# Element-wise work on either of two engines, one weight ring for all chunks, and a rearranged start, in a fused attention and MLP kernel

## The chip, the cores and the metric

The kernel runs on one core of a Trainium2 chip. The metric is the device time of one launch in microseconds. Five engines work side by side, each through its own list of instructions in order: PE (TensorE, matmuls; PEld is its weight load), DVE (VectorE), ACT (ScalarE), POOL (GpSimd) and SP (SyncE, which here only issues DMAs). An instruction that waits for a semaphore holds back everything behind it on its engine.

## The reference

One transformer block on a sequence of 2048 rows and 512 columns, 32 heads of 16, in float32:

```python
mod = (_silu(c) @ w_mod).reshape(c.shape[0], 6, 1, -1)
sa, ca, ga, sb, cb, gb = (mod[:, 0], mod[:, 1], mod[:, 2], mod[:, 3], mod[:, 4], mod[:, 5])
h = _layernorm(x, axis=-1) * (1 + ca) + sa
x = x + ga * _A_ref(h, A_wqkv, A_wo)             # softmax attention, 32 heads, then @ wo
h = _layernorm(x, axis=-1) * (1 + cb) + sb
x = x + gb * _B_ref(h, B_w1, B_w2, B_w3, B_w4)
```

`_B_ref` is two parts with residuals: `gelu(layernorm(x) @ w1)`, whose four column quarters are shifted by 1, -1, 2 and -2 rows and multiplied by `w2`; then `gelu(layernorm(x1) @ w3) @ w4` with 1792 hidden columns. The matrices are scaled up by 8 or 64, so plain bfloat16 products are not accurate enough.

## The kernel before

**Numbers in two parts.** Each matmul operand is kept as a high part and a low part (`hi = Copy(x)` on ACT, `lo = x - hi` by a subtraction), and a product is three matmuls: hi·hi, hi·lo, lo·hi (`mm3`, L322, L324 and L326 of the helper).

**Prologue (about the first 107 us).** The first layer norm, its transposes `hT`, the modulation columns, and the first group of K and Q columns. Q, K and V go to DRAM (`Qs`, `Ks`, `Vs`) and come back per head pair.

**Attention.** The sequence is cut into four chunks of 512 query rows; a chunk has 16 head pairs; a head pair in a chunk is a *unit* (64 units, the `units` list) of 16 key tiles, so there are 1024 steps `s`. A step has for each of two heads:

- `mb` (L939, PE) and `mx` (L935, DVE, `reduce_max` of a 128x512 bank): the row maxima, taken 24 steps ahead (`LEAD`),
- `sc` (L955, PE) and `pt` (L951, ACT, `Exp` into int32): the scores. The maximum is part of the matmul, through rows of `qtl` written by the DMAs `qtl<-nm`,
- the low half of P (`p_low`, L1003): one POOL instruction of 128x1024 for both heads, or two of 128x512 on ACT (`L120` in the profile) when the planner sees POOL more than `LACT` = 800 ns behind ACT,
- `pv` (L1028 high part, L1025 low part, PE).

**Fillers.** Everything else is written as Python generators that yield PE time, and as chains of element-wise steps `("A" | "D" | "G", cost, function)`, with A for ACT, D for DVE and G for POOL. They are: Q, K and V of the later heads; the weights of the MLP and of `wo`, split once into two parts and stored to DRAM as 20 pieces of 1 MB (`pieces_load`, `pieces_gen`; buffers `wst` and `wq`); the modulation rows `garow`, `sbrow`, `cbrow` and `gbrow` (`mod_gen`); and per chunk a `tail`: `wo`, two layer norms, `w1` with gelu, `w2`, `w3` with gelu, `w4`. The tail of the last chunk runs after attention.

**What sets the order.** `Sched` writes the program in the order of a planned time. It has a time for each engine (`T`), a cost for each step (`cA`, `cD`, `cG`: for DVE `n/0.96 + 69` ns, for POOL `2.2 n + 40` ns), and places the fillers between blocks of attention by a budget per step. `misc(e, until)` puts the ready steps of chains into the plan of engine `e`; `crit` places the steps of attention. The order that comes out is fixed in the program; on the chip each engine follows its list and waits on semaphores. The planner's costs are constants: a DVE step has the same cost whatever POOL is doing at that moment. Seven PSUM banks (`NSM`) are shared by scores, maxima and fillers, so a bank that DVE or ACT has not read yet holds up the next matmul.

**Gelu in the attention stage.** Its chain is: ACT square and copy (L1311, L1312), DVE cube (L1316, with one operand in PSUM), ACT tanh and scale (L1320, L1321), POOL product `xs<-xs,sq` (L1322), ACT high part (L1306), POOL low part `g<-xs,g` (L1307). After attention the product is on DVE (L1328) and only the low part on POOL.

**The tail's weights** come through a `Ring` of three 1 MB buffers `wr`, made anew in each `tail`; `get` takes loaded pieces and `more` asks for the next when the matmuls on them are planned.

Of the kernel before, what the change touches and what calls it, by code (L numbers as in the profile page):

```python
# [21 lines left out]
P = 128  # L22
KT = D // P
NKT = S // P
CH = 512
# [33 lines left out]
LACT = 800.0  # L59
WX = 2  # L60
# [4 lines left out]
PLOAD = 3500.0  # L65
WSR = 1
# [10 lines left out]
class Sched:  # L77
# [57 lines left out]
    def misc(self, e, until):  # L135

        while True:
            best = None
            for ch in self.chains:
                if ch[1] and ch[1][0][0] == e:  # L140
                    start = max(self.T[e], ch[0])
                    if ch[3] in self.owner and ch[0] <= max(until, self.T[e]):
                        best = start, ch
                        break
                    if start + ch[1][0][1] <= until + AGE * max(0.0, self.T[e] - ch[0]) and (not best or start < best[0]):
                        best = start, ch
            if not best:
                break
            self.emit(best[1])

    def emit(self, ch):

        e, cost, fn = ch[1].pop(0)
# [140 lines left out]
def kernel(ctx, tc, A_x, A_wqkv, A_wo, B_w1, B_w2, B_w3, B_w4, c, w_mod, out):  # L294
# [7 lines left out]


# [496 lines left out]

    def pieces_load():
        yield lambda: ("v", 0, 2) in done
        for i, (nm, src, nk, n) in enumerate(pieces):
            if i == order["wo"][0]:
                yield lambda: ("vcol", 0) in done and ("vcol", 1) in done
                yield from mod_gen((2, garow, 0.0))
            if i == order["w4"][0]:
                yield lambda: len(wqs) == NWQ and not loaded
                yield from mod_gen((3, sbrow, 0.0), (4, cbrow, 1.0), (5, gbrow, 0.0))
            src3 = kpn(src)  # L810
            for c in range(2):
# [3 lines left out]
                loaded.append((i, nm, c, t, e))  # L815
        loaded.append(None)

    def pieces_gen():
        while True:
# [11 lines left out]
            if nm in rows:  # L831
                ops.append(("G", cG(), lambda f=f, r=rows[nm]: pool.tensor_tensor(f, f, r, op=OP.mult)))
# [5 lines left out]
            def store(i=i, c=c, w=w, f=f, gone=gone):  # L838
                for h, t in enumerate((w.bitcast(F32), f)):
                    e = sch.dma(dma.dma_start, Ws[i][:, h, 512 * c:512 * c + 512], t)  # L840
                sch.after(e, gone)
            sch.chain(*ops, ("A", cA(), lambda f=f, w=w: act.activation(w, f, AF.Copy)),
                      ("G", cG(), lambda f=f, t=t, w=w: pool.tensor_tensor(t, f, w, op=OP.subtract)),
                      (None, 0, store), ready=e)
        yield lambda: len(wqs) == NWQ
# [26 lines left out]
    for g in (mod_cols(), bounds(), ln1_T(), qk_first(hi, lo), weights_gen(), qkv_gen(0, 3), qkv_gen(1, 2, 4, 5, 6)):  # L872
# [118 lines left out]
    def p_low(s):  # L991
# [4 lines left out]
        g, a = [max(sch.T[e], ready) for e in "GA"]  # L996
        if g > a + LACT:
# [12 lines left out]
    def pv_part(s, lo):  # L1010
# [20 lines left out]
        if lo:  # L1031
# [3 lines left out]
            if kt % 4 == 2:  # L1035
                load_v(u + 1, kt // 4)
# [42 lines left out]
    tp = [None, None]  # L1079

    class Ring:


        def __init__(self, ids):
# [3 lines left out]
            self.add(3)  # L1088

        def add(self, n, pl=0):  # L1090

            for _ in range(n):
                if self.n < len(self.ids):
# [3 lines left out]
                    sch.dma(dma.dma_start, w.bitcast(F32), Ws[i])  # L1097
                    self.q.append((halves(w, pieces[i][2]), pl))
# [53 lines left out]
    def tail(ci):  # L1152
# [10 lines left out]
        ids = order["wo"] + order["w1"] + order["w2"]  # L1163
        for f0, nf in FG:
            ids = ids + order["w3"][f0 // 2:(f0 + nf) // 2] + order["w4"][f0 // 2:(f0 + nf) // 2]
        ring = Ring(ids)
# [17 lines left out]
        wo, more = ring.get(2)  # L1184
# [73 lines left out]
        for i, t in enumerate(new):  # L1258
# [16 lines left out]
            def center(xb=xb, x1=x1, m=m, ops=ops):  # L1275
                ops[0][2]()
                sch.late = sch.put("G", 464, sch.T["D"] - cD() + XX, ops[1][2]) + XX
# [5 lines left out]
            go = partial(sch.chain, ("D", cD(), x1_add), ("D", 2 * cD() + 150, center), ("D", cD(), scale), *ops2,  # L1283
# [9 lines left out]
        def gelu(b, n, hi, lo, key):  # L1293
# [8 lines left out]
            def end():  # L1302
# [4 lines left out]
                        ("G", cG(n), lambda: pool.tensor_tensor(lo, xs, hi, op=OP.subtract)), (None, 0, end))  # L1307
            if psd["s"]:
# [6 lines left out]
                def cube():  # L1315
# [6 lines left out]
                          ("G", cG(n), lambda: pool.tensor_tensor(xs, xs, sq, op=OP.mult)), *tail_ops, bank=b)  # L1322
# [21 lines left out]
        for gi, ts in enumerate(grp):  # L1344
# [4 lines left out]
            for half in range(2):  # L1349
                if gi == 0:  # L1350
                    w1.append(ring.get(1))
# [10 lines left out]
        w, more = ring.get(2)  # L1362
# [208 lines left out]
```

## Time and profile before

| | |
|---|---|
| median of 3 runs | 2130.53 us (2129.33 to 2140.78) |
| profiled execution | 2136.83 us, its span 2135.1 us |
| granted PE clock, mean | 0.963 |
| busy: PE, PEld | 1977.7 us (93%), 1163.4 us (54%) |
| busy: DVE, ACT, POOL | 1647.3 us (77%), 1544.9 us (72%), 1708.3 us (80%) |
| DMA | 292.68 MB in 228513 packets |

Busy PE time is a loose measure, since matmuls are pipelined and their ends are modelled. Busy shares over the whole span are means over stages with different limits: the prologue to 107 us, an early part of attention to 499 us in which Q, K, V and the weight pieces are made, the rest of attention to 1945 us, and the last tail. A time in the trace is counted from the start of the span.

### The profile page before, as it was taken

What the parts mean: (1) busy time and instruction counts of PE and PEld (TensorE: products, weight loads), DVE (VectorE), ACT (ScalarE), POOL (GpSimd) and SP (SyncE); (2) the same over time, 40 slices, a digit from 0 to 9 for tenths busy, and PEclk for the clock granted to TensorE, in tenths of its full rate; (3) what the DMA queues carried; (4) which work ended last, traced back from release to release, by engine and by line L of the source; (5) the groups of instructions that cost most, each with busy time, mean ns of one, the idle gap of its engine ahead of it and who ended that gap; (6) DMA issues with size and microseconds to landing.
All of it is one profiled execution on the core that took longest, in us unless ns stands there. A gap on an engine that the chain in (4) does not pass through costs nothing.

```text
span 2135.1 us, 41502 instructions
## 1 busy us (share of the span) xinstructions
PE 1977.7 (93%) x14464; PEld 1163.4 (54%) x14464; DVE 1647.3 (77%) x2936; ACT 1544.9 (72%) x3336; POOL 1708.3 (80%) x1649
## 2 busy tenths in 40 slices
PE   6979898999898999999989999999899999998899
PEld 4645554554343555555444555555545555555788
DVE  6758678788779888878888888788798888861654
ACT  5367777668866878877867897887678887785353
POOL 4378788679987999988968999898779998896441
PEclk9989999999887999999989999999989999999899
DMA  5787867656564344454543444445543434443332
GB/s 193 196 256 222 225 176 204 166 151 167 166 182 99 80 121 105 121 129 124 162 99 68 108 113 124 109 112 124 149 102 82 129 87 107 122 114 118 147 139 84
DMA packets 228513, 292.68 MB, mean 137 GB/s; under 512 B 121264, under 2 KB 172976, under 8 KB 212016
## 3 DMA queue, kind: packets, MB, share of 16 engines
q1 hardware_dynamic: 228304, 290.02, 49.9%
q8 instruction: 115, 1.88, 0.4%
q14 instruction: 94, 0.77, 0.1%
HBM read 226.49 MB, written 62.91 MB: 136 GB/s over the span
## 4 chain that ended last, share of the span: by engine, by line
PE 54%; DVE 14%; ACT 12%; DMA 8%; POOL 7%; issue 3%; SPq 3%; POOLq 0%; ACTq 0%; DVEq 0%
PE mb L939 11%; PE pv L1028 8%; DVE mx L935 8%; PE sc L955 8%; ACT pt L951 6%; PE w L324 5%; PE w L322 5%; PE w L326 5%; POOL pt L1003 4%; PE pv L1025 4%; SPq L99 3%; DMA qtl<-nm 2%; DMA wst<-in_w_mod_dram 1%; DMA wst<-in_B_w_dram 1%; DVE tst L333 1%
## 5 line engine op out<-in xcount | busy, mean ns | idle before, releaser
L935 DVE TENSOR_REDUCE mx<-mb 128x1 f32<-128x512 f32 x2048 | 1280.9, 683 | 208.2 <-PE mb L939 176.5
L1003 POOL TENSOR_SCALAR pt<-pt 128x1024 f16<-128x1024 uint16 x975 | 1300.2, 1367 | 148.1 <-ACT pt L951 145.0
L951 ACT ACTIVATE pt<-sc 128x512 int32<-128x512 f32 x2048 | 1081.7, 607 | 305.5 <-PE mb L939 230.6
L939 PE MATMUL mb<-kst,qtl 48*128 48x512 f32 x2048 | 779.1, 464 | 73.7 <-ACT pt L951 35.9
L955 PE MATMUL sc<-qtl,kst 64*128 64x512 f32 x2048 | 744.4, 456 | 31.7 <-DMA qtl<-nm 16.6
L939 PEld LDWEIGHTS mb<-kst,qtl 48*128 48x128 f32 x2048 | 354.8, 197 | 290.0 <-ACT pt L951 108.8
L955 PEld LDWEIGHTS sc<-qtl,kst 64*128 64x128 f32 x2048 | 344.1, 190 | 202.3 <-ACT pt L951 62.5
L1028 PE MATMUL pv<-pt,vst 128*32 128x512 f16 x4096 | 366.2, 405 | 0.0
L1025 PE MATMUL pv<-pt,vst 128*25 128x512 f16 (+1 forms) x2048 | 214.3, 403 | 0.5 <-POOL pt L1003 0.5
L1028 PEld LDWEIGHTS <-vst 128*32 128x32 bf16 x4096 | 92.1, 96 | 165.0 <-issue 109.7
L322 PE MATMUL w<-A,wr 128*128 128x256 f32 (+2 forms) x576 | 173.4, 301 | 3.2 <-ACT A L316 3.0
L1307 POOL TENSOR_TENSOR g<-xs,g 128x256 fp32r<-128x256 f32 (+2 forms) x144 | 103.8, 722 | 87.7 <-ACT g L1306 87.5
L324 PE MATMUL w<-A,wr 128*128 128x256 f32 (+2 forms) x576 | 172.3, 299 | 1.3 <-DVE A L312 1.1
L326 PE MATMUL w<-A,wr 128*128 128x256 f32 (+2 forms) x576 | 170.1, 295 | 0.0
L322 PEld LDWEIGHTS w<-A,wr 128*128 128x128 f32 x576 | 111.4, 193 | 22.3 <-issue 11.8
L324 PEld LDWEIGHTS w<-A,wr 128*128 128x128 f32 x576 | 111.3, 193 | 19.1 <-issue 16.3
L322 PE MATMUL w<-wr,g 128*128 128x512 f32 x288 | 119.4, 415 | 1.7 <-DVE x L1407 0.9
L326 PE MATMUL w<-wr,g 128*128 128x512 f32 x288 | 118.2, 411 | 0.5 <-POOL g L1307 0.3
L326 PEld LDWEIGHTS w<-A,wr 128*128 128x128 f32 x576 | 111.4, 193 | 10.4 <-issue 10.4
L324 PE MATMUL w<-wr,g 128*128 128x512 f32 x288 | 117.0, 406 | 0.0
L1316 DVE SCALAR_TENSOR_TENSOR sq<-sq,w 128x256 f32<-128x256 f32 (+1 forms) x108 | 43.6, 404 | 81.5 <-ACT xs L1312 67.7
L1407 DVE TENSOR_TENSOR x<-x,w 128x512 f32<-128x512 f32 x64 | 43.7, 683 | 55.6 <-PE w L326 55.5
(145 smaller groups left out, 2239.0 us busy)
## 6 DMA issues: line engine op xcount, KB each, us to landing
wr<-Ws SPq DMA_DIRECT2D x80, 1024.0 KB, 6.2
vst<-Vs SPq DMA_DIRECT2D x256, 192.0 KB, 2.6
kst<-Ks SPq DMA_DIRECT2D x126, 384.0 KB, 6.9
qtl<-Qs SPq DMA_DIRECT2D x128, 96.0 KB, 5.3
Vs<-vt SPq DMA_DIRECT2D x32, 384.0 KB, 5.1
Ws<-wq SPq DMA_DIRECT2D x40, 256.0 KB, 4.5
Ws<-wst SPq DMA_DIRECT2D x40, 256.0 KB, 4.8
wst<-in_B_w_dram SPq DMA_DIRECT2D x36, 256.0 KB, 5.0
```

Source lines behind the costliest of these rows:

```text
L99: start(o, i)
L322: te.matmul(o, lh, rh, start=first, stop=False)
L324: te.matmul(o, lh, rl, start=False, stop=False)
L326: te.matmul(o, ll, rh, start=False, stop=last)
L935: end = sch.crit("D", 605, e + PX, lambda: dve.reduce_max(mxs[u][:, j, g, c:c + 1], b, axis=AX.X))
L939: return ready, lambda: te.matmul(b, lhs, kst[u % 3][r, c * CH:(c + 1) * CH], start=True, stop=True), after
L951: ea = sch.crit("A", 480, e + PX, lambda: act.activation(pt[s][:, j], b, AF.Exp))
L955: return ready, lambda: te.matmul(b, kst[u % 3][r, kt * P:(kt + 1) * P], qst[u][r], start=True, stop=True), after
L1003: e_low[s] = XP["G"] + sch.crit("G", 1345, ready, lambda: pool.tensor_scalar(o, i, 0.5, 1.0, op0=OP.mult, op1=OP.mult))
L1025: te.matmul(acc[r:r + n, :], v[:, (kt + i) % 4, c - n:c].bitcast(F16), pt[s + i].bitcast(F16)[:, j, 0::2], start=False, stop=kt == NKT - 2 ...
L1028: te.matmul(acc[r:r + 32, :], v[:, kt % 4, r:r + 32], pt[s].bitcast(F16)[:, j, 1::2], start=kt == 0, stop=False, skip_group_check=True)
L1307: ("G", cG(n), lambda: pool.tensor_tensor(lo, xs, hi, op=OP.subtract)), (None, 0, end))
```

## The change

- **Either engine.** A step of a chain may name two engines, `"DG"`, with a cost for each. `misc` of either engine may take it. Both engines use the same instruction, `tensor_tensor`. Written so: the low part of gelu, the product of gelu in the attention stage, the product with the modulation row and the low part in `pieces_gen`, and the last two steps on `xb` and `x` behind `w2`. All of them have both operands in SBUF.
- **Low halves of P.** `p_low` has a first choice: if POOL is planned more than `LDVE` = 800 ns behind DVE, the instruction goes to DVE.
- **Own power step.** The `pow` on POOL inside the layer norm was emitted from within the DVE step `center`; it is now a step of the chain.
- **Ring through chunks.** One `Ring` for all four chunks, so the next chunk's first pieces are asked for when the last ones are given back. `get` now waits, during attention, for the planned landing plus `WLAT` = 4000 ns. `more` asks 300 ns later. The loads of V (`load_v`) are asked for 300 ns later too.
- **Later MLP weights.** `pieces_load` starts after `("kq", 2)` and not after `("v", 0, 2)`; a piece's chain is ready 4000 ns later. Q, K and V generators run one after the other and not in two lines.
- **List of modulation rows.** `mod_rows` makes the four rows, in a generator of its own.

Core of the diff:

```diff
@@ misc, emit
-                if ch[1] and ch[1][0][0] == e:
+                if ch[1] and e in (ch[1][0][0] or ""):
...
+    def cost(self, ch, e):
+
+        es, cost, _ = ch[1][0]
+        return cost[es.index(e)] if len(es) > 1 else cost
...
+    def either(fn, n=CH):
+        eng = {"D": dve, "G": pool}
+        return "DG", (cD(n), cG(n)), lambda e: fn(eng[e])
@@ pieces
+    def mod_rows():
+        yield lambda: ("kq", 1) in done
+        yield from mod_gen((2, garow, 0.0))
+        done.add("garow")
...
     def pieces_load():
-        yield lambda: ("v", 0, 2) in done
+        yield lambda: ("kq", 2) in done
...
-                loaded.append((i, nm, c, t, e))
+                loaded.append((i, nm, c, t, e + WLAT))
...
-                ops.append(("G", cG(), lambda f=f, r=rows[nm]: pool.tensor_tensor(f, f, r, op=OP.mult)))
+                ops.append(either(lambda e, f=f, r=rows[nm]: e.tensor_tensor(f, f, r, op=OP.mult)))
...
-                      ("G", cG(), lambda f=f, t=t, w=w: pool.tensor_tensor(t, f, w, op=OP.subtract)),
+                      either(lambda e, f=f, t=t, w=w: e.tensor_tensor(t, f, w, op=OP.subtract)),
...
-    for g in (mod_cols(), bounds(), ln1_T(), qk_first(hi, lo), weights_gen(), qkv_gen(0, 3), qkv_gen(1, 2, 4, 5, 6)):
+    for g in (mod_cols(), bounds(), ln1_T(), qk_first(hi, lo), weights_gen(), qkv_gen(0), qkv_gen(1, 2, 3, 4, 5, 6)):
@@ p_low
-        g, a = [max(sch.T[e], ready) for e in "GA"]
-        if g > a + LACT:
+        g, a, d = [max(sch.T[e], ready) for e in "GAD"]
+        if g > d + LDVE:
+            e_low[s] = XP["D"] + sch.crit("D", 660, ready, lambda: dve.tensor_scalar(
+                o, i, 0.5, 1.0, op0=OP.mult, op1=OP.mult))
+        elif g > a + LACT:
...
-                load_v(u + 1, kt // 4)
+                sch.after(e + 300, partial(load_v, u + 1, kt // 4))
@@ Ring
         def get(self, n):
-            ws, pls = zip(*self.q[:n])
+            yield lambda: len(self.q) >= n and (sch.T["P"] >= self.q[n - 1][2] or not psd["s"])
+            ws, pls, _ = zip(*self.q[:n])
             del self.q[:n]
-            return ws, lambda: [self.add(1, p) for p in pls]
+            def more():
+                for p in pls:
+                    sch.after(sch.T["P"] + 300, partial(self.add, 1, p))
+            return ws, more
...
-        ring = Ring(ids)
+            rings.append(Ring(ids * NC))
+        ring = rings[0]
@@ layer norm behind wo
-            go = partial(sch.chain, ("D", cD(), x1_add), ("D", 2 * cD() + 150, center), ("D", cD(), scale), *ops2,
+            go = partial(sch.chain, ("D", cD(), x1_add), ops[0], ("D", cD(), center), ops[1], ("D", cD(), scale), *ops2,
@@ gelu
-                        ("G", cG(n), lambda: pool.tensor_tensor(lo, xs, hi, op=OP.subtract)), (None, 0, end))
+                        either(lambda e: e.tensor_tensor(lo, xs, hi, op=OP.subtract), n), (None, 0, end))
...
-                          ("G", cG(n), lambda: pool.tensor_tensor(xs, xs, sq, op=OP.mult)), *tail_ops, bank=b)
+                          either(lambda e: e.tensor_tensor(xs, xs, sq, op=OP.mult), n), *tail_ops, bank=b)
@@ behind w2
-                          ("G", cG(), lambda xb=xb: pool.tensor_tensor(xb, xb, gbrow, op=OP.mult)),
-                          ("G", cG(), lambda xb=xb, x1=x1: pool.tensor_tensor(x1, x1, xb, op=OP.add)),
+                          either(lambda e, xb=xb: e.tensor_tensor(xb, xb, gbrow, op=OP.mult)),
+                          either(lambda e, xb=xb, x1=x1: e.tensor_tensor(x1, x1, xb, op=OP.add)),
```

The instructions on PE, and the DMAs, are the same in number in both programs. Over the whole program 328 element-wise `tensor_tensor` instructions go from POOL to DVE and 14 of these kinds stay; 45 low halves of P leave ACT (90 instructions of half the size), 43 of them for POOL and two for DVE. The order shows it at three places.

DVE in the attention stage, in the tail of chunk 0 (units 23 and 24), before; `mx` is the row maximum, `sq<-sq,w` the cube of gelu, and `x<-x,w` adds the product with `w4`:

```order
L935 TENSOR_REDUCE mx<-mb 128x1 x3
L985 TENSOR_REDUCE mf<-mx 128x8
L935 TENSOR_REDUCE mx<-mb 128x1 x6
L1316 SCALAR_TENSOR_TENSOR sq<-sq,w_10814 128x256
L935 TENSOR_REDUCE mx<-mb 128x1 x3
L1316 SCALAR_TENSOR_TENSOR sq<-sq,w_10951 128x256
L935 TENSOR_REDUCE mx<-mb 128x1 x5
L1316 SCALAR_TENSOR_TENSOR sq<-sq,w_10988 128x256
L935 TENSOR_REDUCE mx<-mb 128x1 x6
```

The same engine in the tail of chunk 0 of the changed program (unit 23), where `g<-xs,g` is the low part and `xs<-xs,sq` the product of gelu:

```order
L961 TENSOR_REDUCE mx<-mb 128x1 x3
L1343 TENSOR_TENSOR g_10515<-xs,g_10515 128x256
L961 TENSOR_REDUCE mx<-mb 128x1 x3
L1358 TENSOR_TENSOR xs<-xs,sq 128x256
L961 TENSOR_REDUCE mx<-mb 128x1
L1352 SCALAR_TENSOR_TENSOR sq<-sq,w_10776 128x256
L961 TENSOR_REDUCE mx<-mb 128x1 x2
L1011 TENSOR_REDUCE mf<-mx 128x8
L1343 TENSOR_TENSOR g_10515<-xs,g_10515 128x256
L961 TENSOR_REDUCE mx<-mb 128x1 x3
L1358 TENSOR_TENSOR xs<-xs,sq 128x256
```

Each gelu tile now puts three instructions between the maxima where it put one; the other two came from POOL.

POOL where the pieces of `w4` are split, before (`pt` is the low half of P, `wst` and `wq` the two parts of a piece):

```order
L1003 TENSOR_SCALAR pt_622<-pt_622 128x1024
L843 TENSOR_TENSOR wst_115<-wst_115,wq_121 128x512
L1003 TENSOR_SCALAR pt_623<-pt_623 128x1024
L832 TENSOR_TENSOR wst_114<-wst_114,gbrow 128x512
L1003 TENSOR_SCALAR pt_625<-pt_625 128x1024
L832 TENSOR_TENSOR wst_117<-wst_117,gbrow 128x512
L1003 TENSOR_SCALAR pt_627<-pt_627 128x1024
```

DVE at its first pieces of `w4` in the changed program:

```order
L961 TENSOR_REDUCE mx<-mb 128x1 x3
L857 TENSOR_TENSOR wst_116<-wst_116,gbrow 128x512
L961 TENSOR_REDUCE mx<-mb 128x1 x3
L869 TENSOR_TENSOR wst_116<-wst_116,wq_121 128x512
L869 TENSOR_TENSOR wst_117<-wst_117,wq_119 128x512
L961 TENSOR_REDUCE mx<-mb 128x1 x3
L857 TENSOR_TENSOR wst_118<-wst_118,gbrow 128x512
```

The product with the row and the low part went from between the low halves on POOL to between the maxima on DVE.

SP at the change from chunk 0 to chunk 1, before (`out_dram<-x` stores finished rows, `wr<-Ws` loads a piece):

```order
L99 DMA out_dram<-x_7710 128x512
L99 DMA qtl_612<-Qs 48x512
L99 DMA kst_614<-Ks 48x2048
L99 DMA qtl_612<-Qs 48x512
L99 DMA kst_614<-Ks 48x2048
L99 DMA wr<-Ws_87 128x2048
L99 DMA wr<-Ws_88 128x2048
L99 DMA wr<-Ws_78 128x2048
L99 DMA x_14502<-in_A_x_dram 128x512
```

and in the changed program, ahead of the stores:

```order
L101 DMA wr<-Ws_97 128x2048
L101 DMA wr<-Ws_87 128x2048
L101 DMA vst_620<-Vs 128x768
L101 DMA vst_617<-Vs 128x768
L101 DMA qtl_612<-nm 1x128x2 x8
L101 DMA wr<-Ws_88 128x2048
```

The two pieces of `wo` for chunk 1 (`Ws_87`, `Ws_88`) moved from behind the last stores of chunk 0 to ahead of them.

More of the change, by code (lines that the diff above doesn't have):

```diff
@@ L1183, in tail @@
             sch.chain(*[("G", 990, partial(copy, k)) for k in range(KT)], mark(("g", ci)))
-        wo, more = ring.get(2)
+        wo, more = yield from ring.get(2)
         banks = {}
@@ L1361, in tail @@
         SH = (1, -1, 2, -2)
-        w, more = ring.get(2)
+        w, more = yield from ring.get(2)
         for si, ts in enumerate(sub):
@@ L1383, in tail @@
             g2 = []
-            w3 = [ring.get(1) for _ in range(nf // 2)]
+            w3 = []
             for si, ts in enumerate(sub):
@@ L1396, in tail @@
                         more()
-            w, more = ring.get(nf // 2)
+            w, more = yield from ring.get(nf // 2)
             for si, ts in enumerate(sub):
```

56 lines of the change are left out of this document (36 added, 20 removed).

## The prediction, on record before the changed kernel was run

> **What bounds the kernel now.** I read the page's busy line first, then the windows by stage, then windows of single units, then the groups and the waits. From the page:
>
> ```profile
> PE 1977.7 (93%) x14464; PEld 1163.4 (54%) x14464; DVE 1647.3 (77%) x2936; ACT 1544.9 (72%) x3336; POOL 1708.3 (80%) x1649
> ```
>
> PE's 93% is modelled and says little. The three others are all near 75 to 80%, so the stage decides. The windows by stage (columns: window, its length, then busy us of PE, PEld, DVE, ACT and POOL with their instructions, granted clock, DMA share, GB/s):
>
> ```profile
> 107.00:499.00 392.00, 355.63 (x2658) 205.56 (x2654) 291.66 (x507) 273.80 (x566) 312.83 (x265) 0.97 0.72 199
> 499.00:1945.00 1446.00, 1369.12 (x10482) 753.44 (x10479) 1183.11 (x2088) 1138.26 (x2474) 1282.57 (x1233) 0.97 0.46 117
> 1945.00:2136.00 191.00, 168.17 (x924) 144.27 (x922) 92.81 (x175) 79.75 (x195) 67.85 (x94) 0.95 0.34 129
> ```
>
> The stage from 499 to 1945 us, "the long stage", is two thirds of the time. In it POOL is busy 1282.57 of 1446 us, 88.7%, DVE 81.8%, ACT 78.7%. Single stretches show both ways in which it is bound:
>
> ```profile
> 535.00:562.00 27.00, 24.09 (x172) 10.43 (x170) 21.83 (x37) 24.25 (x49) 26.71 (x24) 0.94 0.59 174
> 621.00:653.00 32.00, 30.10 (x207) 16.16 (x203) 29.62 (x53) 19.79 (x39) 23.23 (x22) 1.00 0.30 66
> 653.00:686.00 33.00, 28.80 (x182) 13.00 (x182) 31.27 (x57) 22.34 (x42) 25.69 (x30) 0.74 0.42 110
> 1103.00:1134.00 31.00, 26.22 (x181) 11.67 (x181) 30.72 (x55) 22.36 (x42) 24.52 (x28) 0.83 0.45 116
> ```
>
> From 535 us POOL is full (99%) and a unit with next to no filler takes 27 us. In the other three DVE is the fullest, 93%, 95% and 99%, and where it passes 93% the clock granted to PE falls to 0.74 and 0.83. So POOL bounds much of this stage, DVE the places behind `wo`.
>
> **A price the planner does not know.** The 12 instances of the `scale` step (L1281, a DVE instruction with two operands in SBUF) that lie in attention, all its 16, one of them with the two low halves around it, and the other such group (L422):
>
> ```profile
> L1281 DVE SCALAR_TENSOR_TENSOR xb<-xb,trs,sbrow x12: 1027/1610/1812, 637.9 to 1586.1; 128x512 f32<-128x512 f32 x12
> L1281 DVE SCALAR_TENSOR_TENSOR xb<-xb,trs,sbrow x16: 742/1540/1812, 637.9 to 1995.9; 128x512 f32<-128x512 f32 x16
> L1281 DVE SCALAR_TENSOR_TENSOR xb<-xb,trs,sbrow x1: 1546/1546/1546, 648.2 to 648.2; 128x512 f32<-128x512 f32 x1
> L1003 POOL TENSOR_SCALAR pt<-pt x2: 1338/1570/1801, 647.9 to 649.2; 128x1024 f16<-128x1024 uint16 x2
> L422 DVE TENSOR_TENSOR wp<-wst,wp x14: 674/924/1782, 48.5 to 365.6; 128x512 fp32r<-128x512 f32 x14
> ```
>
> (Durations are least, median, most.) Alone it takes 742 ns; beside POOL 1610. The low half that began at 647.9 ends at 649.24; the DVE instruction begun at 648.2 ends at 649.75, half a microsecond later, and the next low half takes 1801 ns and not 1338. Each engine waits out the other's instruction. All 328 moved instructions have two operands in SBUF and meet low halves on POOL.
>
> **The change, part by part.** By the order, 232 moved instructions lie in the long stage (31 of 512 columns, 174 of 256, 27 of 128), 42 of 512 before it, 54 after attention. Their prices, on POOL and on DVE, and those of the low halves:
>
> ```profile
> L1003 POOL TENSOR_SCALAR pt<-pt 128x1024 f16<-128x1024 uint16 x975 | 1300.2, 1367 | 148.1 <-ACT pt L951 145.0 <-POOL nm L988 0.4
> L120 ACT ACTIVATE pt<-pt 128x512 f16<-128x512 uint16 x98 | 70.3, 806 | 0.0
> L1307 POOL TENSOR_TENSOR g<-xs,g 128x256 fp32r<-128x256 f32 x116 | 83.2, 718 | 68.3 <-ACT g L1306 68.1
> L1322 POOL TENSOR_TENSOR xs<-xs,sq 128x256 f32<-128x256 f32 x94 | 69.6, 742 | 8.9 <-ACT sq L1321 8.8
> L1307 POOL TENSOR_TENSOR g<-xs,g 128x128 fp32r<-128x128 f32 x14 | 6.4, 464 | 2.4 <-ACT g L1306 2.4
> L843 POOL TENSOR_TENSOR wst<-wst,wq 128x512 fp32r<-128x512 f32 x40 | 52.2, 1305 | 7.9 <-ACT wq L842 7.8
> L1407 DVE TENSOR_TENSOR x<-x,w 128x512 f32<-128x512 f32 x64 | 43.7, 683 | 55.6 <-PE w L326 55.5
> L1316 DVE SCALAR_TENSOR_TENSOR sq<-sq,w 128x256 f32<-128x256 f32 x94 | 39.6, 421 | 73.2 <-ACT xs L1312 61.3 <-POOL pt L1003 9.3 <-ACT mf L986 1.9
> L1316 DVE SCALAR_TENSOR_TENSOR sq<-sq,w 128x128 f32<-128x128 f32 x14 | 4.0, 287 | 8.3 <-ACT xs L1312 6.4 <-POOL pt L1003 0.7 <-ACT mf L986 0.7
> L422 DVE TENSOR_TENSOR wp<-wst,wp 128x512 fp32r<-128x512 f32 x14 | 13.8, 994 | 2.3 <-ACT wp L424 2.3
> ```
>
> *POOL in the long stage.* Off: 31 x 1.305 = 40, 174 x 0.73 = 127, 27 x 0.464 = 13. On: 30 low halves (of the 43 it gains) x 1.367 = 41, and where a DVE instruction holds up a low half up to 0.46 us (1801 less 1338) for 512 columns; taken as 0.35 for half of 232: 40. So 1282.6 - 180 + 81 = 1184, 82%. *ACT* loses 76 of its 90 half-size instructions here, 76 x 0.806 = 61, and goes to 1077, 74%.
>
> *DVE in the long stage.* Without waits: 31 x 0.683 = 21, 174 x 0.421 = 73, 27 x 0.287 = 8, two low halves about 2 (no row; between 0.68 for as many bytes and POOL's 1.37 each). 1183.1 + 104 = 1287, 89.0%: just the load that POOL has now. Then the waits. Bounds by rows: none where POOL happens to rest; 0.32 for L422 (its mean, in the last row, less 674); 0.87 for L1281 in attention, which comes right behind POOL's power step and so often meets a fresh low half. A moved instruction follows ACT, not POOL, so it meets POOL at any point: POOL at work 82% of the time, on average half of 1.367 us left, less some 0.25 us by which the quoted pair overlaps (742 less 500 ns): 0.82 x 0.43 = 0.36, a little more because the wait is never below nothing. That gives about 0.4, near L422, and I take it: 232 x 0.4 = 93, DVE 1380 us, 95.4% of the present stage.
>
> *From load to time.* PE works in order, and its next maxima need the bank that DVE has not read. POOL's queue is looser: the low half is used by matmuls two blocks later. Were the fullest engine again full to 88.7%, the stage would take 1380 / 0.887 = 1556 us, +110; at the 95% of the stretch from 653 us, 1453, +7. That stretch had the slow clock, the one at 93% did not; I take 91%: 1516, **+70 us**.
>
> *The early part.* DVE gets 42 x (0.683 + 0.4) = 45 and is at 337 of 392 us, 86%, no bound yet; POOL loses 42 x 1.305 = 55 and gains 13 x 1.367 = 18 and 42 x 0.35 = 15. What binds here are waits (two rows of waits between 107 and 499 us, and the first window of that part):
>
> ```profile
> ACT wq L842 <- DMA wst<-in_B_w_dram: 20.8, 12, 4.7
> PE mb L939 <- ACT pt L951: 19.6, 9, 9.3
> 107.00:160.00 53.00, 38.05 (x266) 22.80 (x263) 29.12 (x51) 32.06 (x68) 38.89 (x33) 0.87 0.86 255
> ```
>
> ACT stands before a piece that has not landed, with `Exp` behind it, and PE behind that for up to 9.3 us. Readiness 4 us later and pieces after `("kq", 2)`, past the first three units, should take most of it, and some clock with it: **-20 us** (from 0, if ACT meets other late loads, to -27: all 19.6 and half of what the clock withholds, 0.13 x 53 = 7).
>
> *The ring.* The same matmul list, asked for earlier:
>
> ```profile
> PE wo L322 <- DMA wr<-Ws: 10.1, 2, 5.2
> ```
>
> Two chunk changes (1535 and 1969 us) wait 5 us each; the piece now lands before: **-10** (0 to -10). On SP the earlier `wr` stands ahead of `vst` and `qtl` loads and of stores, and waits for PE to free a buffer; 16 steps of slack for `vst` cover it, and without them a late `vst` stops `pv`. The 300 ns on V's loads, the power step and the list of rows: nothing, under the same slack and under the early fillers.
>
> *The end.* The order puts 47 matmuls of 512 columns and 20 of 256 more behind the last `pv`. Matmuls of 512 in that stage follow each other at (1981.85 - 1977.09) / 21 = 0.227 us:
>
> ```profile
> 1977.09 0.39 PE L324 MATMUL wo<-wr,A 128*128 128x512 f32 x1
> 1981.85 0.39 PE L324 MATMUL wo<-wr,A 128*128 128x512 f32 x1
> ```
>
> 47 x 0.227 = 11, the 20 at about half, 2 to 3: **+14 us**. DVE has room there (92.8 of 191 us), and with POOL empty nothing waits.
>
> Sum: 70 - 20 - 10 + 14 = +54 on the profiled execution's 2136.8 us (span 2135.1), so 2191; that execution was 6.3 above the median of 2130.5, which gives 2185 for the median.
>
> **A page's rule beside it.** The Trainium skill ("SBUF — State Buffer", section "Who interferes with whom") says that DVE's second SBUF input and GpSimd's reads share one port pair under an exclusive lock, held for the whole instruction, so the later one fully blocks. The trace agrees that each waits for the other, but 742 ns of work ended 0.5 us after the lock was free, so some 0.25 us of it had run before. The case of no overlap is the third rival.
>
> **Rivals.** *DVE packs (faster).* Mechanism: DVE, one list with ready work always behind, fills to 95% as from 653 us, and the wait is L422's 0.32. 1287 + 74 = 1361, / 0.95 = 1433, -13; with the early gain full, -13 - 27 - 10 + 14 = -36, a median of 2094. For it: 27 us of POOL at 99% cost no clock below 0.94. Against: the clock at 653 us. At 91% full it turns at a wait of 0.19 us, at 95% at 0.44.
>
> *A wash.* Wait and packing cancel against early gain and ring: within 10.7 us (0.5% of 2130.5, about what a measurement of this kernel can tell from no change).
>
> *Full block.* No overlap: 0.82 x 0.68 = 0.56 each, 130 us, DVE 1417, at 91% 1557, +111; sum +95, 2226 for the median. If the instructions bunch as L1281 does (0.87), DVE is at 1489, more than the stage has now; at 95% 1567, +105 with all the rest.
>
> *"By which has room" does not balance.* It may seem that the choice protects DVE. The order says no: 328 of 342 go to DVE, since its planned cost is lower and the wait is not in it. This is in the forecast.
>
> **Numbers.** Forecast (slower, about +54) 0.45; full block or bunching 0.22; packing 0.22; a wash 0.11. Faster by over 0.5%: 0.22; within: 0.11; slower: 0.67. The range for 8 in 10 runs from the packing case, 2090, to 2280, past the full block (2226) and toward the bound of 88.7% full (1556, +110 and the rest: 2225) with full block (1417 / 0.887 = 1598, +152: 2267). The forecast's own range is 2150 to 2225.
>
> **What the profile after would show.** Moved groups on DVE at 256 columns with a mean near 0.8 us, not 0.42, and a median of low halves on POOL above 1.36; DVE at 92% or more of the long stage, POOL near 80%; more of PE's waits at DVE's `mx`; no PE wait for `wr`; ACT's wait for `wst` mostly gone. It is wrong if the moved groups stay near 0.45 us, or if the long stage takes 1446 us or less with DVE above 93%.

## The result, and the profile after

The changed kernel takes 2161.37 us (2157.78 to 2165.36) where the kernel before takes 2135.66 on the same chip: a ratio of 1.0112, interval 1.0089 to 1.0134, some 25 us slower. Its profiled execution took 2160.27 us, its span 2158.5. The direction and the mechanism are the forecast's; the size is half of it.

The busy line, the chain's shares by engine and the two costliest groups, from the page of the changed kernel:

```profile
PE 2002.0 (93%) x14464; PEld 1180.1 (55%) x14464; DVE 1868.6 (87%) x3266; ACT 1497.4 (69%) x3246; POOL 1537.6 (71%) x1364
...
PE 48%; DVE 32%; ACT 6%; DMA 6%; issue 3%; POOL 2%; SPq 2%; ACTq 0%; POOLq 0%; DVEq 0%
...
L1032 POOL TENSOR_SCALAR pt<-pt 128x1024 f16<-128x1024 uint16 x1018 | 1378.5, 1387 | 313.4 <-ACT pt L977 307.9
L961 DVE TENSOR_REDUCE mx<-mb 128x1 f32<-128x512 f32 x2048 | 1279.0, 680 | 106.1 <-PE mb L965 90.0
```

DVE and POOL have changed places: 87% and 71% where they had 77% and 80%. In the chain that ended last, DVE had 14% before:

```profile
PE 54%; DVE 14%; ACT 12%; DMA 8%; POOL 7%; issue 3%; SPq 3%; POOLq 0%; ACTq 0%; DVEq 0%
```

To compare the stages, both kernels are cut at the same events: the first `sc` of attention, the first of the thirteenth unit, and the last `pv`. These cuts lie some us from the prediction's rounder ones, so the rows of before stand here too. Windows by stage (window, length, busy us of PE, PEld, DVE, ACT and POOL, clock, DMA share, GB/s), first of before, then of the changed kernel:

```profile
101.00:488.00 387.00, 351.11 (x2600) 203.93 (x2601) 286.90 (x499) 269.64 (x557) 307.60 (x261) 0.96 0.72 198
488.00:1951.00 1463.00, 1385.59 (x10628) 761.81 (x10626) 1193.77 (x2105) 1150.86 (x2500) 1297.02 (x1244) 0.97 0.46 118
1951.00:2136.00 185.00, 162.17 (x858) 140.79 (x858) 92.07 (x173) 75.69 (x186) 62.52 (x90) 0.94 0.35 133
```

```profile
100.00:471.00 371.00, 339.20 (x2525) 193.19 (x2524) 315.89 (x529) 261.41 (x544) 292.65 (x242) 0.95 0.74 202
471.00:1970.00 1499.00, 1410.82 (x10637) 777.38 (x10636) 1366.39 (x2346) 1110.40 (x2419) 1187.99 (x1031) 0.97 0.45 115
1970.00:2159.00 189.00, 172.27 (x928) 151.40 (x927) 111.64 (x235) 76.90 (x192) 15.86 (x36) 0.95 0.36 137
```

The early part is 16 us shorter, the long stage 36 longer, the end 4 longer: +24, the whole difference. In the long stage DVE is busy 91.2% of the time and POOL 79%; before it was POOL with 88.7% and DVE with 82%. The granted clock is 0.97 in both.

The moved instructions, by form (busy us, then mean ns of one), and those of the long stage up to 1965 us by line (least, median, most), in the changed kernel:

```profile
L1343 DVE TENSOR_TENSOR g<-xs,g 128x256 fp32r<-128x256 f32 x114 | 79.6, 699 | 5.7 <-ACT g L1342 5.0
L1358 DVE TENSOR_TENSOR xs<-xs,sq 128x256 f32<-128x256 f32 x90 | 76.6, 851 | 9.8 <-ACT sq L1357 9.7
L869 DVE TENSOR_TENSOR wst<-wst,wq 128x512 fp32r<-128x512 f32 x38 | 41.0, 1080 | 0.0
L1343 DVE TENSOR_TENSOR g<-xs,g 128x384 fp32r<-128x384 f32 x14 | 7.7, 552 | 0.0
```

```profile
L1343 DVE TENSOR_TENSOR g<-xs,g x99: 245/795/1516, 655.1 to 1960.7; 128x256 fp32r<-128x256 f32 x85, 128x128 fp32r<-128x128 f32 x14
L1358 DVE TENSOR_TENSOR xs<-xs,sq x97: 277/886/1552, 666.2 to 1962.9; 128x256 f32<-128x256 f32 x84, 128x128 f32<-128x128 f32 x13
```

An instruction of 256 columns, 421 ns of work, takes about twice that in attention. After attention, with POOL nearly empty, one of 384 columns takes only 552 ns.

The waits of the changed kernel (who waits, for whom: us, times, longest):

```profile
POOL pt L1032 <- ACT pt L977: 307.9, 363, 6.6
PEld mb L965 <- DVE mx L961: 92.0, 225, 2.3
DVE mx L961 <- PE mb L965: 90.0, 169, 2.0
ACT wp L440 <- DMA wst<-in_A_wqkv_dram: 17.5, 7, 6.6
PE mr L619 <- DMA wst<-in_w_mod_dram: 10.1, 3, 6.8
```

and of before:

```profile
DVE mx L935 <- PE mb L939: 176.5, 291, 8.9
PEld mb L939 <- DVE mx L935: 77.4, 178, 1.4
POOL pt L1003 <- ACT pt L951: 145.0, 182, 8.6
```

POOL now stands idle for a new P twice as long as before (307.9 against 145.0 us), DVE stands idle for a new bank half as long, and PE waits more often for DVE to read one.

### The profile page after: what moved, and what is told of

It reads as the page before. It is cut to its first block, busy times and chain, and to the rows that moved or that the text cites. A ratio compares the mean times of both kernels' runs of the same rounds, so it can differ in the third digit from the quotient of the medians.

```text
span 2158.5 us, 42214 instructions
## 1 busy us (share of the span) xinstructions
PE 2002.0 (93%) x14464; PEld 1180.1 (55%) x14464; DVE 1868.6 (87%) x3266; ACT 1497.4 (69%) x3246; POOL 1537.6 (71%) x1364
## 4 chain that ended last, share of the span: by engine, by line
PE 48%; DVE 32%; ACT 6%; DMA 6%; issue 3%; POOL 2%; SPq 2%; ACTq 0%; POOLq 0%; DVEq 0%
DVE mx L961 18%; PE mb L965 10%; PE pv L1057 7%; PE sc L981 7%; PE w L338 5%; PE w L342 5%; PE w L340 5%; ACT pt L977 4%; PE pv L1054 3%; DVE xs L1358 3%; DVE g L1343 2%; SPq L101 2%; DMA kst<-Ks 1%; POOL pt L1032 1%; DMA wst<-in_A_wqkv_dram 1%
## 5 line engine op out<-in xcount | busy, mean ns | idle before, releaser
L1032 POOL TENSOR_SCALAR pt<-pt 128x1024 f16<-128x1024 uint16 x1018 | 1378.5, 1387 | 313.4 <-ACT pt L977 307.9
L965 PE MATMUL mb<-kst,qtl 48*128 48x512 f32 x2048 | 787.7, 468 | 79.0 <-ACT pt L977 19.9
L1054 PE MATMUL pv<-pt,vst 128*17 128x512 f16 (+1 forms) x2048 | 215.9, 406 | 1.0 <-POOL pt L1032 1.0
L338 PE MATMUL w<-A,wr 128*128 128x256 f32 (+2 forms) x576 | 176.0, 306 | 0.4 <-ACT A L332 0.3
L340 PE MATMUL w<-A,wr 128*128 128x256 f32 (+2 forms) x576 | 173.4, 301 | 0.3
L342 PE MATMUL w<-A,wr 128*128 128x256 f32 (+2 forms) x576 | 172.1, 299 | 0.0
L338 PEld LDWEIGHTS w<-A,wr 128*128 128x128 f32 x576 | 113.5, 197 | 19.0 <-issue 13.5
L340 PEld LDWEIGHTS w<-A,wr 128*128 128x128 f32 x576 | 113.2, 196 | 16.9 <-issue 15.6
L342 PEld LDWEIGHTS w<-A,wr 128*128 128x128 f32 x576 | 113.1, 196 | 12.7 <-issue 12.7
L1343 DVE TENSOR_TENSOR g<-xs,g 128x256 fp32r<-128x256 f32 (+2 forms) x142 | 96.3, 680 | 6.4 <-ACT g L1342 5.5
L1358 DVE TENSOR_TENSOR xs<-xs,sq 128x256 f32<-128x256 f32 (+1 forms) x103 | 86.3, 839 | 10.3 <-ACT sq L1357 10.0
L1265 POOL TENSOR_TENSOR trs<-tmv,mhalf 128x1 f32<-128x1 f32 x48 | 31.4, 654 | 78.8 <-DVE tmv L1262 78.8
```

The costliest lines, as they stand in the source:

```text
L338: te.matmul(o, lh, rh, start=first, stop=False)
L340: te.matmul(o, lh, rl, start=False, stop=False)
L342: te.matmul(o, ll, rh, start=False, stop=last)
L965: return ready, lambda: te.matmul(b, lhs, kst[u % 3][r, c * CH:(c + 1) * CH], start=True, stop=True), after
L1032: e_low[s] = XP["G"] + sch.crit("G", 1345, ready, lambda: pool.tensor_scalar(o, i, 0.5, 1.0, op0=OP.mult, op1=OP.mult))
L1054: te.matmul(acc[r:r + n, :], v[:, (kt + i) % 4, c - n:c].bitcast(F16), pt[s + i].bitcast(F16)[:, j, 0::2], start=False, stop=kt == NKT - 2 ...
```

## The experiments

The theory: the choice gives nearly every step to DVE; each such step also waits there for POOL's low half; DVE becomes the engine that sets the long stage; start and ring give a little back. Its rivals: the choice is harmless and something else costs; or it is the plain load and not the wait. All ratios are to the kernel before on the same chip, with a 95% interval.

### Start, ring and power step kept, the choice of engine taken away

```diff
-        return "DG", (cD(n), cG(n)), lambda e: fn(eng[e])
+        return "G", cG(n), lambda: fn(pool)
```

> The changed kernel with every step that may choose put back on POOL (342 on POOL, none on DVE); ring, start, power step and the choice for the low halves stay. Load theory (the moved instructions, with some 0.41 us of wait each, fill DVE): DVE in the long stage falls from 1363 us to about 1200, POOL goes back to about 1290, the gains of the ring and the start remain, and the time is about 2136 - 26 = 2110 us, a ratio of 0.988 to before. Rival theory (the moved instructions cost nothing that matters; ring and rearranged start lost the time): it stays at about 2161 us, ratio 1.012, or above, since POOL is full again.

Measured: 2107.87 us, ratio 0.9867 (0.983 to 0.9903). The loss comes from the choice: without it the change is a gain of 31 us by the medians, 28 by the ratio. Its long stage:

```profile
475.00:1939.00 1464.00, 1398.66 (x10752) 776.29 (x10750) 1220.37 (x2136) 1135.15 (x2479) 1305.79 (x1248) 0.98 0.47 120
```

POOL is the fullest again, 1305.79 of 1464 us, 89.2%. The stage has the length that it had before, but more matmuls lie in it (10752 against 10628) and so fewer behind it: the rest of the gain is a shorter early part and end. Twenty low halves went to DVE by `p_low`'s new first choice, and beside POOL they took from 729 to 3348 ns, 1470 on the average, where the two of the changed kernel took 774. By form, here and then in the changed kernel:

```profile
L1024 DVE TENSOR_SCALAR pt<-pt 128x1024 f16<-128x1024 uint16 x20 | 29.4, 1470 | 1.2 <-ACT pt L977 1.2
```

```profile
L1024 DVE TENSOR_SCALAR pt<-pt 128x1024 f16<-128x1024 uint16 x2 | 1.5, 774 | 0.6 <-ACT pt L977 0.6
```

### The kernel before, with the choice of engine alone

```diff
+    def either(fn, n=CH):
+        eng = {"D": dve, "G": pool}
+        return "DG", (cD(n), cG(n)), lambda e: fn(eng[e])
...
-                        ("G", cG(n), lambda: pool.tensor_tensor(lo, xs, hi, op=OP.subtract)), (None, 0, end))
+                        either(lambda e: e.tensor_tensor(lo, xs, hi, op=OP.subtract), n), (None, 0, end))
```

(and the same at the five other places, with `misc`, `cost` and `emit` as in the change)

> The kernel before with the choice of engine alone (338 instructions go to DVE); ring, start and low halves as before. Load theory: DVE in the long stage rises from 1193 us by about 100 of work and 97 of waiting, less 27 of overlap, to about 1363; at 91% full the stage takes some 1490 instead of 1459, and without the gains of ring and start the time is about 2136 + 45 = 2180 us, ratio 1.02. Rival theory: 2136 us or a little below, ratio 1.000 or less.

Measured: 2199.09 us, ratio 1.0274 (1.0245 to 1.0303), +60, more than expected. Windows by stage:

```profile
104.00:507.00 403.00, 368.81 (x2600) 209.33 (x2596) 325.02 (x541) 266.25 (x551) 287.46 (x238) 0.92 0.73 203
507.00:2007.00 1500.00, 1400.68 (x10576) 762.55 (x10577) 1356.78 (x2343) 1118.50 (x2429) 1175.71 (x1019) 0.96 0.43 110
2007.00:2200.00 193.00, 171.11 (x908) 150.23 (x906) 110.24 (x231) 75.64 (x189) 15.40 (x36) 0.93 0.34 132
```

The long stage is 37 us longer than before and DVE 90.5% full: the same as in the changed kernel. The early part is 16 us longer, which the prediction had priced at nothing; DVE is at 81% there, so load is not what binds, and the granted clock is 0.92 against 0.96. With the new start beside it the choice costs nothing early (377 us with the new start alone, below, and 371 in the changed kernel), though not in every order of steps: the run with the price alone, further below, has the new start too and takes 393 us there. Why the choice costs time with the old start is not settled.

### Start alone

The kernel before with `mod_rows`, `pieces_load` after `("kq", 2)`, `WLAT` in `loaded`, and the generators one after the other.

```diff
-        yield lambda: ("v", 0, 2) in done
+        yield lambda: ("kq", 2) in done
...
-                loaded.append((i, nm, c, t, e))
+                loaded.append((i, nm, c, t, e + WLAT))
```

> The kernel before with the start alone: pieces after the third K group and ready 4000 ns later, the generator of modulation rows, Q, K and V one after the other. By the prediction's term: ACT's 20.8 us of waits for pieces go and PE's 19.6 us behind them, 2139 to about 2119 us, ratio 0.991. Rival (the same work is only late, and POOL, full after it, gives it back): 0.998 to 1.005, with a shorter early part and a longer one behind it.

Measured: 2122.59 us, ratio 0.9918 (0.9894 to 0.9942). Its early part, and its waits for loads:

```profile
103.00:480.00 377.00, 345.89 (x2550) 197.86 (x2547) 285.26 (x494) 275.06 (x570) 313.79 (x269) 0.95 0.74 207
```

```profile
ACT wp L425 <- DMA wst<-in_A_wqkv_dram: 15.7, 7, 6.7
PE wo L323 <- DMA wr<-Ws: 9.8, 2, 5.3
PE mr L604 <- DMA wst<-in_w_mod_dram: 8.3, 3, 6.7
ACT wq L853 <- DMA wst<-in_B_w_dram: 1.6, 2, 1.1
```

ACT's wait for the pieces went from 20.8 us to 1.6, as expected. Other loads are late in its place: for `A_wqkv` and `w_mod` the waits of before were these:

```profile
ACT wp L424 <- DMA wst<-in_A_wqkv_dram: 5.7, 6, 2.9
PE mr L603 <- DMA wst<-in_w_mod_dram: 1.7, 4, 0.9
```

They rose to 15.7 and 8.3 us. By the medians the run is 14 us faster, by the ratio 18, and between 12 and 23 by its interval, so the expected 20 is not excluded. In the trace the early part is 10 us shorter (377 against 387).

### Ring alone

```diff
-        ring = Ring(ids)
+        if not rings:
...
+            rings.append(Ring(ids * NC))
+        ring = rings[0]
```

(with `get` and `more` as in the change)

> The kernel before with the ring through chunks alone (with its 4000 ns and 300 ns). By the prediction's term: PE's two waits for wr (10.1 us) go, 2139 to 2129 us, ratio 0.995. Rival (the earlier loads hold up other loads on SP and give it back): 1.000 or above.

Measured over ten runs: 2135.41 us, ratio 0.9978 (0.9957 to 1.0). PE waits for `wr` nowhere any more, so the mechanism is as forecast, but the 10 us arrive in part at most: 5 us by the ratio, 1 by the medians. Of the rival, loads held up on SP, the trace shows one new wait of PE for `vst`, of 2.4 us. The windows:

```profile
101.00:497.00 396.00, 355.88 (x2599) 206.99 (x2598) 287.00 (x498) 269.72 (x557) 307.52 (x261) 0.95 0.69 193
497.00:1943.00 1446.00, 1375.52 (x10578) 756.26 (x10576) 1190.10 (x2101) 1154.66 (x2511) 1287.37 (x1236) 0.97 0.47 118
1943.00:2135.00 192.00, 170.10 (x909) 149.06 (x907) 94.02 (x177) 76.78 (x190) 62.52 (x90) 0.94 0.35 133
```

The long stage is 17 us shorter, but the early part 9 longer and the end 7 longer: matmuls moved from the long stage to behind it (909 against 858), and the early part lost by a cause that these runs do not show.

### The wait taken away, first try

The changed kernel, with a POOL instruction that only writes in place of the low half. The low half of P is left out.

```diff
-            e_low[s] = XP["G"] + sch.crit("G", 1345, ready, lambda: pool.tensor_scalar(
-                o, i, 0.5, 1.0, op0=OP.mult, op1=OP.mult))
+            e_low[s] = XP["G"] + sch.crit("G", 1345, ready, lambda: (pool.memset(o, 0.0), pool.memset(o[:, 0:384], 0.0)))
```

> The changed kernel with the low half of P left out: POOL writes zeros by two memsets of 1024 and 384 columns (about the same time by the row of the 1536-column memset, 1413 ns), so it still waits for Exp but reads nothing from SBUF. DVE's list is the same. Wait theory (the cost is the time DVE stands before POOL's reads): the moved groups of 256 columns fall from a mean of 0.83 us to 0.42, DVE in the long stage from 1363 to about 1266 us, and the time by 60 to 100 us, to 2060 to 2100. Rival (the added instructions themselves or the order cost the time, the wait is absorbed): the groups get shorter but the time stays within 15 us of 2161. If a memset holds the port as a read does, the groups stay at 0.83 us and nothing changes.

Measured: 2222.99 us, ratio 1.0396 (1.0372 to 1.0419): a miss of the experiment itself. Three groups by form, and the window of the long stage:

```profile
L1032 POOL MEMSET pt<- 128x1024 f16 x1018 | 1285.2, 1263 | 20.8 <-ACT pt L977 20.6
L1032 POOL MEMSET pt<- 128x384 f16 x1018 | 545.8, 536 | 58.6
L1342 DVE TENSOR_TENSOR g<-xs,g 128x256 fp32r<-128x256 f32 x114 | 47.5, 418 | 9.3 <-ACT g L1341 8.2
```

```profile
483.00:2033.00 1550.00, 1420.27 (x10638) 778.75 (x10637) 1275.07 (x2346) 1108.89 (x2424) 1484.08 (x1862) 0.96 0.43 112
```

The waits are gone (418 ns), and DVE falls to 1275 us. But the two fills take 1263 + 536 = 1799 ns where the low half took 1387, and POOL, at 95.7% of the stage, took the place of DVE. So it says nothing yet on what the waits cost.

### The wait taken away, with POOL no slower

The same with one fill. The low half of P is left out.

```diff
+            e_low[s] = XP["G"] + sch.crit("G", 1345, ready, lambda: pool.memset(o, 0.0))
```

> As the run without reads, with one memset of 1024 columns (1262 ns there, where a low half takes 1357) and not two, so that POOL is no fuller than in the changed kernel. The low half of P is left out. Wait theory: moved groups at 0.42 us, DVE in the long stage about 1363 - 97 = 1266 us, POOL about 1100; the time falls from 2161 to between 2060 and 2100 us, ratio 0.965 to 0.982. Rival (the wait is absorbed and the instructions' own 100 us or the order cost the time): 2145 to 2165 us.

Measured: 2070.07 us, ratio 0.9669 (0.9641 to 0.9696), 91 us below the changed kernel. The fill, two moved groups, and the long stage:

```profile
L1032 POOL MEMSET pt<- 128x1024 f16 x1018 | 1249.1, 1266 | 353.8 <-ACT pt L977 350.1
L1342 DVE TENSOR_TENSOR g<-xs,g 128x256 fp32r<-128x256 f32 x114 | 47.4, 417 | 5.9 <-ACT g L1341 4.8
L1357 DVE TENSOR_TENSOR xs<-xs,sq 128x256 f32<-128x256 f32 x90 | 37.5, 417 | 10.7 <-ACT sq L1356 10.3
```

```profile
468.00:1883.00 1415.00, 1359.27 (x10640) 756.93 (x10639) 1268.39 (x2347) 1104.54 (x2419) 1081.99 (x1031) 0.99 0.47 122
```

The same order of instructions, without the waits: DVE is busy 98 us less, the stage is 84 us shorter, and DVE is again 89.6% full. So the wait, and not the moved work by itself, is what makes the change slower. (This kernel is also 38 us below the one that has no step on DVE, 2107.87, but that comparison is not an even one: there POOL is the fullest, and a shorter instruction would help it too.) Two things changed besides: POOL's instruction is 0.12 us shorter, which should not bind with POOL at 76%; and the matmuls of the low half multiply zeros. The granted clock is 0.99 here, against 0.97 in the changed kernel; in the first try, with the same zeros, it was 0.96, so the zeros alone do not explain it. How much of the 84 us the clock gave is not separated. The run also agrees with the Trainium skill ("SBUF — State Buffer", section "Who interferes with whom"), by which a DVE instruction with two SBUF inputs contends with a GpSimd instruction that reads SBUF, not with one that only writes it: 417 ns beside the fills against 699 and 851 beside the low halves.

### The wait in the planner's price, and a true balance

First the price alone: DVE's cost of such a step is 415 ns higher, about the mean wait that the trace of the changed kernel gives (in its long stage the means are 1083, 831 and 700 ns for 512, 256 and 128 columns, less 683, 421 and 287 alone: 408 ns over all of them).

```diff
-        return "DG", (cD(n), cG(n)), lambda e: fn(eng[e])
+        return "DG", (cD(n) + 415.0, cG(n)), lambda e: fn(eng[e])
```

> The changed kernel with 415 ns added to DVE's price of a step that may choose, and nothing else: DVE is still asked first, and takes 235 and not 328. Load theory: time goes with DVE's load, and the load falls by about 90 x 0.8 = 70 us over the run, so about 2161 - 60 = 2100 us if the removed ones all lie in the long stage, 2125 if half of them do. Rival (the order was wrong because the price was, the load itself is harmless): about 2088 us, as with the balanced choice, although DVE has 150 more to do than there.

Measured over ten runs: 2138.27 us (2124.68 to 2148.64), ratio 0.9983 (0.9956 to 1.001). 235 steps still go to DVE. `misc` hands a step to whichever engine asks for one first, and the price only says whether it still fits into that engine's plan. The time is above the 2100 to 2125 expected: the long stage and the end together are some 41 us shorter than in the changed kernel, but the early part, 393 us, is 22 longer, for a cause that the runs do not show. The long stage:

```profile
494.00:1978.00 1484.00, 1410.71 (x10707) 777.60 (x10707) 1327.33 (x2306) 1114.78 (x2440) 1216.65 (x1085) 0.96 0.45 116
```

Then both: the price, and a rule that an engine takes a step only if the plan has it finish there first.

```diff
-                if ch[1] and e in (ch[1][0][0] or ""):
+                if ch[1] and e in (ch[1][0][0] or "") and self.mine(ch, e):
...
+    def mine(self, ch, e):
+        es, cost, _ = ch[1][0]
+        if len(es) == 1:
+            return True
+        f = {x: max(self.T[x], ch[0]) + y for x, y in zip(es, cost)}
+        return f["D"] < f["G"] if e == "D" else f["G"] <= f["D"]
```

> The changed kernel in which a step goes to the engine that the planner sees finish it first, with 415 ns of waiting added to DVE's price; 84 go to DVE, 258 to POOL. Load theory: DVE in the long stage at about 1193 + 84 x 0.8 = 1250 us or less, POOL at about 1270, neither over 88%; with the gains of ring and start the time is about 2100 to 2110 us, ratio 0.985. Rival theory (ring and start lost the time): 2150 to 2160 us.

Measured: 2088.07 us, ratio 0.9762 (0.9734 to 0.9791), faster than both kernels; 84 steps go to DVE. Part of this is the new start and ring: below the kernel that has them too and leaves every step on POOL (2107.87) it is 20 us, 1.1% by the two ratios. The long stage:

```profile
478.00:1908.00 1430.00, 1371.01 (x10672) 763.56 (x10671) 1242.88 (x2176) 1111.77 (x2434) 1283.87 (x1199) 0.98 0.47 119
```

POOL 89.8%, DVE 86.9%: both close to full, and the stage 33 us shorter than before. Three variants take it apart. The rule without the price (`cD(n)`):

> The balanced choice without the 415 ns in DVE's price: 203 go to DVE and 139 to POOL (with them 84 and 258). Load theory: 119 more on DVE at some 0.8 us, about 95 us more load there, gives 2088 + 30 to 60, 2120 to 2150 us. Rival (it is the rule 'whoever finishes first' that helps, not the wait in the price): within 10 us of 2088.

2126.55 us, ratio 0.9962 (0.9947 to 0.9978), 203 steps on DVE. Of the changed kernel's time the price alone takes off 23 us, the rule alone 35, both together 73. The rule with more than twice the wait (`cD(n) + 900.0`):

> The balanced choice with 900 ns in DVE's price: 30 go to DVE, 312 to POOL. Load theory: POOL has about 54 x 0.75 = 40 us more than in the balanced run and is the fullest again, DVE about as before; 2095 to 2108 us, toward the run with all on POOL (2108). Rival (every instruction kept from DVE helps): 2080 us or less.

2098.31 us, ratio 0.9829 (0.9807 to 0.9852), 30 steps on DVE. And the rule with the price of 415, with low halves given to DVE at any lead (`LDVE = 0.0`):

> The balanced choice (415 ns) with the low halves going to DVE as soon as POOL is planned behind it at all: 28 and not 2 on DVE, 8 half-size ones on ACT and not 26. In the run with all on POOL a low half on DVE took 1470 ns, and its price in the planner is 660. Load theory: DVE gets 26 x 1.4 = 36 us, of which 14 x 0.83 = 12 come off again, POOL loses about as much: within 10 us of 2088, rather above. Rival (POOL is what still binds): 2075 or less.

2098.13 us (2095.28 to 2118.16), ratio 0.9848 (0.98 to 0.9896): nothing is gained by giving DVE 28 low halves where it had two (70 steps go to DVE here).

The other kernels that have the new start and ring and compute the low half, in the order of how many steps go to DVE (the kernel before takes 2135.66 to 2138.9 us on the chips that ran them):

| steps on DVE | 0 | 30 | 84 | 203 | 235 | 328 (the change) |
|---|---|---|---|---|---|---|
| us | 2107.87 | 2098.31 | 2088.07 | 2126.55 | 2138.27 | 2161.37 |

The fastest of these has a quarter of them there. The kernels also differ in rule and price, so the count alone need not be what orders them. One number is common to them: in the long stage the fullest engine of DVE and POOL is at 88.2 to 91.2% in every kernel of this document but the one with the two fills, whichever engine that is. In these the stage is as long as its fullest engine's time divided by about 0.9.

## Why the prediction came out as it did

**What held.** The wait: the moved instructions of the long stage (236 in the trace) are on the average 0.41 us longer than alone, against 0.4 forecast, and the mean of 512 columns is 1083 ns against 0.683 + 0.4. The bound: DVE at 91.2% of the long stage, against 91%; no row gave the 91, which was picked between 88.7 and 95, so that it is this close is in part luck. POOL: 109 us less than before in the long stage, against 99. That the choice does not balance: 328 of 342 steps on DVE. Of the signs named, three missed: DVE is at 91.2% and not at 92 or more; POOL's low halves have a higher mean (1387 against 1367 ns) but their median, 1357, is not above 1.36; and of ACT's waits for `wst` those for the MLP's pieces went, but 17.5 us for `A_wqkv` came up.

**The rivals.** Full block would give 0.56 us per instruction, bunching 0.87; the measured 0.41 is below both. Packing needed DVE at 95%; no kernel here brought DVE above 91.2%, and only POOL, in the first try with the fills, reached 95.7%.

**The step that failed: DVE's load in the long stage, 104 + 93 = 197 us.** By durations of records it is right: the records of DVE in the two long stages, added up from the traces, give 1326 us before and 1526 after, 200 more. But the 1183 us to which the prediction added it (1194 in the present cut) is busy time, in which moments covered by two records count once. Records of neighbouring DVE instructions overlap, which the page shows in the row of `mx`: 2048 x 680 ns is 1393 us, busy time 1279. In the long stage the overlap is 132 us before and 159 after, so 27 of the 200 us are counted twice, and busy time rose by 173. The run with one fill tells in which part: without the wait DVE is busy 1268 us, 75 more than before where the forecast had 104 for the work alone, and with it 98 more, where the forecast had 93. So the term that was too large is the 104 of added work, not the wait. 27 / 0.91 is 30 us of stage: +70 should have been +40. Then 40 - 20 - 10 + 14 = +24 is the difference of the two spans, but in part by luck, since the smaller terms are off too, and cancel:

- *Start, -20.* -16 in the early part of the trace; alone -14 by the medians and -18 by the ratio. ACT's wait for the pieces went, as priced; the waits for `A_wqkv` and `w_mod` that took its place (17.5 and 10.1 us in the changed kernel) were named as a bound, "if ACT meets other late loads", and not in the sum. (The bound of -27 also adds the whole 0.13 x 53 = 7 us, where the text says half.)
- *Ring, -10.* The two waits went, the time followed in part at most: alone -1 us by the medians, -5 by the ratio, its interval from -9 to 0. That the fuller engines had caught up during PE's wait, so that it cost little, would fit, but is only argued.
- *The end, +14.* +4. The matmuls came as the order said (928 against 858 in the records), but PE's busy share rose from 162.17 of 185 us to 172.27 of 189, 88% to 91%. POOL, which had 62.52 us of work there, has 15.86, and the low part of gelu of 384 columns takes 552 ns on DVE, where it took 1015 on POOL (row below), so PE may wait less for it; but with the choice alone, POOL as empty, the end took 193 us for 908 matmul records, at a clock of 0.93, so this is not shown.

```profile
L1307 POOL TENSOR_TENSOR g<-xs,g 128x384 fp32r<-128x384 f32 x14 | 14.2, 1015 | 17.0 <-ACT g L1306 17.0
```

**What does not add up.** By the medians, the choice alone costs 60 us and start and ring alone bring 15: +45, but the change costs 25. By the ratios it is 59 - 18 - 5 = +36 against 24, where the four intervals together leave some 10 us either way. In the traces the difference lies in the early part: 16 us longer with the choice alone, 10 shorter with the start alone, 9 longer with the ring alone, but 16 shorter with all of them. Why is open. The later loads of V, the power step and the choice for the low halves were not run alone.

## What to carry to other kernels

A choice between two engines needs the price of what the engines do to each other, measured, and it needs a rule by which the step goes where it ends first; against the kernel that leaves every step on POOL, one without the other cost about 1% here, and both took off 1.1%. Before adding moved work to an engine's busy time, compare a group's count times mean with its busy time: where the product is larger, records overlap, and part of what is added will vanish in the overlap. And measure how full the fullest engine gets (here 88 to 91%, whichever it was), since a planned load divided by that share tells the length of a stage to some 2%, as long as that share holds: with the two fills it was 95.7%.

## What the runs showed of the hardware

- A DVE instruction with two SBUF operands loses 0.41 us on the average beside POOL instructions of 1.38 us that keep POOL busy 79% of the time, and nothing beside POOL instructions that only write (417 and 418 ns).
- In the changed kernel 61 moved gelu steps of 256 columns began while a low half ran on POOL and met no second one: 56 of them ended 0.19 to 0.23 us after that low half did, where they take 0.42 alone. For 512 and 128 columns the medians are 0.48 (0.68 alone) and 0.08 (0.29 alone). So some 0.2 us of the instruction, whatever its size, is done by then, and the rest comes after; the prediction had read 0.25 from one pair.
- The low half of P, 128x1024 from 16-bit integers to 16-bit floats, takes 774 ns on DVE (two records) and 1387 on POOL; but on DVE, too, it took 1470 ns on the average in the run in which twenty of them lay beside a POOL that was 89% busy, though it has one operand. Fills that only write did not free it: of the two in the run with one fill per step, one took 783 ns and one 1874.
- A fill of 128x1024 16-bit elements on POOL, written to every second place, takes 1263 to 1266 ns, little less than the 1387 of the low half that also reads; 384 columns take 536.
